# Moving the q and k transposes of an attention kernel from TensorE to the DMA crossbar

## The chip, the cores and the metric

One core of one Trainium2 chip. The metric is the device time of one execution in microseconds (us). A kernel is run several times; where a program runs on one core, a run counts as "slow" when it is over 1.5% above the fastest of its kernel, else as "fast".

## The reference

Two layers in one program. The attention (8 batches, 8 heads, 576 tokens, 64 features) adds a coarse attention over means of four tokens to a local one with a band of three neighbours on each side; its output x (4608 x 512) goes through a feed-forward layer with exact Gelu.

```python
q_d = q.reshape(B, H, S // 4, 4, D).mean(axis=3)         # k_d, v_d likewise
out_up = np.repeat(softmax_attention(q_d, k_d, v_d), 4, axis=2)
out_local = softmax_attention(q, k, v, mask=abs(i - j) < 4)
x = (out_up + out_local).transpose(0, 2, 1, 3).reshape(B * S, H * D)
out = gelu(x @ w_in) @ w_out                              # d_ff = 2048, float32 out
```

## The kernel before

All matmuls are fp16. The scores need q and k with the features on the partitions, so both are transposed. Before, each 256-byte row of a head is loaded for itself, with tokens on the partitions, and TensorE transposes blocks of 96 tokens x 2 heads against an identity into PSUM, from where VectorE copies them.

```python
def load_qk(b):                       # 2 x 6 DMAs, runs of 64 float32 = 256 bytes
    for nm, src in (("qn", q), ("kn", k)):
        for c in range(NCK):
            nc.gpsimd.dma_start(out=nat6(ld[b % 2][nm])[:, c, :, :],
                in_=src[b, :, CH * c:CH * c + CH, :].rearrange("h s d -> s h d"))
            yield
...
def t_in(b, p, which):                # one pair of heads
    nat = nat6(ld[b % 2]["qn" if which == "q" else "kn"])
    tr = ppool.tile([128, 1024], F16, tag="tr", name=f"tr_{which}")
    for c in range(NCK):
        nc.tensor.transpose(tr[:, CH * c:CH * c + CH], nat[:, c, 2 * p:2 * p + 2, :], I128[0:CH, 0:CH])
    if which == "q":
        nc.vector.tensor_copy(out=qT[:, p, :], in_=tr[:, 0:S])
        ...                           # GpSimd: sums of four tokens into qd
    else:
        ...                           # VectorE: two copies into kz, two sums into kdz
```

The feed-forward layer is woven into the attention. In each of nine chunks, `m1(c)` is 64 matmuls of the first product (16 groups of four, each closed by a Gelu on ACT; two PSUM banks take turns), and `m2(c)` is 64 of the second. The transposes of batch b = c + 1 stand between the matmuls of m1(c) ("first stage"), its attention between those of m2(c) ("second stage"); `f1(n)` and `f2(n)` issue the next n matmuls.

```python
elif b < B:
    v_down(b)                         # GpSimd: sums of four rows of v
    for p in range(NP):
        f1(6 if p == 0 else 7)
        t_in(b, p, "q")
        f1(7)
        t_in(b, p, "k")
    k_lo()
f1()
...                                   # attn(b, f2, ...), f2()
if b + 1 < B:
    run(load_qk(b + 1))
    run(load_v(b + 1))
```

The softmax here doesn't subtract the row's maximum and nothing guards it: scores larger than these inputs give would overflow.

## Time and profile before

| | before |
|---|---|
| time, median of the first 3 runs (lowest to highest) | 350.56 us (350.33 to 351.19) |
| span in the profile, mean granted clock | 348.4 us, 1.00 |
| TensorE busy | 97% of the span |
| one batch (first + second stage) | 15.89 + 20.33 = 36.22 us |

In the profile, PE is TensorE, PEld its weight loads, DVE VectorE, POOL GpSimd, SP the queue that issues DMAs. "The chain of waits" is followed back from the last instruction to what released it. L200 is a line of the kernel file. The lines themselves stand in the prediction below. The granted clock is the share of its full speed at which TensorE was let run. A DMA's landing is counted from its issue to the arrival of its last bytes. In the kernel, qT and kz hold the transposed q and k, qd and kdz their sums over four tokens, gT the results of Gelu, and out_sb what a store sends out.

### The profile page before, as it was taken

The numbers are of one execution on the slowest core, as the hardware profiler recorded it, in microseconds if no ns is written. First come the engines' busy times: TensorE is split into PE (matmuls) and PEld (weight loads), VectorE is DVE, ScalarE is ACT, GpSimd is POOL, SyncE is SP. The second block draws the span as 40 slices with busy tenths as digits, with TensorE's granted clock in tenths as the row PEclk, the third lists the DMA queues.
The fourth block names the chain that finished last, engine by engine and source line by source line (L and its number), as shares of the span: only waits on it lengthen the run. The fifth ranks groups of instructions, "written<-read, shape, count | busy, mean of one in ns | idle before, by whom it ended". The sixth has DMA issues, their size and how long they took to land.

```text
span 348.4 us, 7162 instructions
## 1 busy us (share of the span) xinstructions
PE 339.0 (97%) x2976; PEld 193.9 (56%) x2976; DVE 184.5 (53%) x338; ACT 192.8 (55%) x360; POOL 180.4 (52%) x243
## 2 busy tenths in 40 slices
PE   8898998999999999999999999999999999999996
PEld 4773455655665566555655575556655664444444
DVE  7793645747574857386747665676558470000000
ACT  3664465645764577357746764566556755614620
POOL 8957649633977298628963797369652000000000
PEclk9999999999999999999999999999999999999999
DMA  6999999920999099908990599129940001011002
GB/s 87 165 205 144 185 164 110 182 75 0 98 159 146 2 77 152 176 0 59 154 171 23 36 148 178 41 18 150 159 79 0 32 33 59 2 60 60 0 34 89
DMA packets 126543, 32.31 MB, mean 93 GB/s; under 512 B 109616, under 2 KB 122032, under 8 KB 126512
## 3 DMA queue, kind: packets, MB, share of 16 engines
q0 software_dynamic: 121184, 22.43, 82.2%
q1 hardware_dynamic: 5328, 9.44, 7.6%
q8 instruction: 23, 0.38, 0.4%
q14 instruction: 8, 0.07, 0.1%
HBM read 44.83 MB, written 9.44 MB: 156 GB/s over the span
## 4 chain that ended last, share of the span: by engine, by line
PE 88%; DMA 6%; DVE 2%; POOL 2%; issue 1%; ACT 0%; POOLq 0%
PE m_ps L224 35%; PE m_ps L200 33%; PE sc L348 4%; DMA w_in_sb<-in_moe_w_in_dram 3%; PE av L403 2%; PE tr_o L441 2%; DMA q_nat<-in_q_dram 2%; PE tr_k L237 2%; PE tr_q L237 2%; DMA k_nat<-in_k_dram 1%; DVE kz L272 1%; PE av L397 1%; PE sc L353 1%; PE m_ps L215 1%; PE av L395 1%; DVE kdz L275 1%
## 5 line engine op out<-in xcount | busy, mean ns | idle before, releaser
L200 PE MATMUL m_ps<-xT,w_in_sb 128*128 128x512 f16 x568 | 133.3, 379 | 0.5 <-ACT gT L195 0.5
L224 PE MATMUL m_ps<-w_out_sb,gT 128*128 128x512 f16 x560 | 130.3, 379 | 0.0
L203 ACT ACTIVATE gT<-m_ps 128x512 f16<-128x512 f32 x142 | 84.8, 597 | 56.7 <-PE m_ps L200 56.7
L200 PEld LDWEIGHTS <-w_in_sb 128*128 128x128 f16 x568 | 52.1, 97 | 54.7 <-issue 0.8
L224 PEld LDWEIGHTS <-gT 128*128 128x128 f16 x560 | 51.9, 98 | 54.6
L228 ACT COPY out_sb<-m_ps 128x512 f32<-128x512 f32 x35 | 20.6, 589 | 42.8 <-PE m_ps L224 37.8
L243 POOL TENSOR_TENSOR q_t<-qT 128x288 f32<-128x288 f16 x24 | 16.0, 667 | 52.0 <-DVE qT L240 37.8
L104 POOL DMA_DIRECT2D q_nat<-in_q_dram x42 | 32.6, 789 | 8.1 <-DMA w_out_sb<-in_moe_w_out_dram 5.7
L252 DVE TENSOR_REDUCE kdz<-kz 64x144 f16<-64x576 f16 x48 | 35.9, 747 | 1.5
L445 DVE TENSOR_TENSOR xT<-tr_o,xd 128x576 f16<-128x576 f16 x28 | 21.2, 758 | 26.9 <-ACT xd L444 26.9
L104 POOL DMA_DIRECT2D k_nat<-in_k_dram x42 | 32.2, 778 | 6.3 <-DMA w_in_sb<-in_moe_w_in_dram 3.5
L418 DVE TENSOR_TENSOR nall<-av,rr 128x896 f16<-128x896 f32 x29 | 31.7, 1091 | 1.0
L248 DVE COPY kz<-tr_k 64x576 f16<-64x576 f16 x48 | 21.9, 455 | 18.2 <-PE tr_k L237 17.5
L381 DVE TENSOR_TENSOR e<-e,band 128x1152 f16<-128x1152 f16 x28 | 21.0, 751 | 17.6 <-ACT e L375 17.6
L219 DVE COPY out_sa<-m_ps 128x256 f32<-128x256 f32 x2 | 0.8, 424 | 54.9 <-PE m_ps L215 54.9
L116 POOL DMA_DIRECT2D v_win<-in_v_dram x30 | 26.6, 912 | 0.0
L348 PE MATMUL sc<-qT,kz 128*128 128x112 f16 (+1 forms) x320 | 25.6, 214 | 0.0
L373 ACT ACTIVATE e<-sc 128x680 f16<-128x680 f32 x32 | 23.4, 732 | 2.0 <-PE sc L348 2.0
L348 PEld LDWEIGHTS <-kz 128*128 128x128 f16 x320 | 21.6, 97 | 0.9
L311 POOL TENSOR_TENSOR v_t<-v_grp 128x1024 f32<-128x1024 f16 x6 | 12.7, 2118 | 17.0 <-DMA v_grp<-in_v_dram 17.0
L444 ACT COPY xd<-tr_o 128x144 f16<-128x144 f16 x28 | 7.7, 276 | 22.0 <-PE tr_o L441 22.0
L375 ACT ACTIVATE e<-sc 128x472 f16<-128x472 f32 x32 | 18.2, 569 | 0.0
(168 smaller groups left out, 407.6 us busy)
## 6 DMA issues: line engine op xcount, KB each, us to landing
out_dram<-out_sb SPq DMA_DIRECT2D x35, 256.0 KB, 3.2
v_win<-in_v_dram POOLq DMA_DIRECT2D x40, 128.0 KB, 9.6
q_nat<-in_q_dram POOLq DMA_DIRECT2D x42, 96.0 KB, 3.7
k_nat<-in_k_dram POOLq DMA_DIRECT2D x42, 96.0 KB, 4.2
v_grp<-in_v_dram POOLq DMA_DIRECT2D x6, 512.0 KB, 8.8
w_in_sb<-in_moe_w_in_dram POOLq DMA_DIRECT2D x4, 512.0 KB, 8.1
w_out_sb<-in_moe_w_out_dram POOLq DMA_DIRECT2D x4, 512.0 KB, 9.4
v_lo<-in_v_dram POOLq DMA_DIRECT2D x6, 64.0 KB, 8.8
```

The lines of the kernel that those rows point to most:

```text
L104: nc.gpsimd.dma_start(out=nat6(ld[b % 2][nm])[:, c, :, :], in_=src[b, :, CH * c:CH * c + CH, :].rearrange("h s d -> s h d"))
L116: nc.gpsimd.dma_start(out=L["vw"][:, j, :, 0:64], in_=v[b, :, W0[j]:W0[j] + 128, :].rearrange("h s d -> s h d"))
L200: nc.tensor.matmul(out=ps, lhsT=w_in_sb[:, fc, 128 * j:128 * j + 128], rhs=xT[:, fc, 512 * c:512 * c + 512], start=(fc == 0), stop=(fc == 3))
L203: nc.scalar.activation(out=g[:, j, :], in_=ps, func=ACTF.Gelu)
L224: nc.tensor.matmul(out=ps, lhsT=g[:, j, 128 * t:128 * t + 128], rhs=w_out_sb[:, j, :], start=(j == 0), stop=(j == NJ - 1))
L248: nc.vector.tensor_copy(out=kz[r, p, hh, :], in_=tr[r, 0:S])
L252: nc.vector.tensor_reduce(out=kdz[r, p, hh, :], in_=kz[r, p, hh, :].rearrange("p (g r) -> p g r", r=4), axis=AX.X, op=ALU.add)
L348: nc.tensor.matmul(out=dst, lhsT=kz[:, p, hh, W0[j]:W0[j] + 128], rhs=qT[:, p, Q0[j]:Q0[j] + QW[j]], start=(b > 0), stop=True)
L373: nc.scalar.activation(out=e2[:, :, 0:340], in_=sc2[:, :, 0:340], func=ACTF.Exp, scale=0.125)
L381: nc.vector.tensor_tensor(out=e2, in0=e2, in1=band.unsqueeze(1).broadcast_to([128, 2, S]), op=ALU.mult)
L418: nc.vector.tensor_tensor(out=nall.rearrange("p j a c -> p a j c"), in0=av4[:, :, :, 0:64], in1=rr.unsqueeze(3).broadcast_to([128, 2, 7, 6 ...
L445: nc.vector.tensor_tensor(out=xT[:, p, S * b:S * b + S].rearrange("p (g r) -> p g r", r=4), in0=tr[:, 0:S].rearrange("p (g r) -> p g r", r=4),
```

## The change

The intent: take the 48 groups of transposes of batches 2 to 7 off TensorE, the bound, and replace 256-byte loads by 1.5 KB ones. Each partition now loads six consecutive tokens of a head (1536 bytes). VectorE regroups them so that a block of 128 columns is two heads of one of the six tokens. One DMA crossbar transpose each for q and k (a DMA that transposes what it moves) turns the whole 96 x 3072 array. Copies then bring the columns into token order: ACT does two of q's four, GpSimd two, VectorE all of k's. The transposes get the SP queue for themselves; the stores, all but the last two, move to ACT's. gT gets one buffer in place of two to make room.

```diff
+    def load_raw(b):
+        for nm, src in (("kn", k), ("qn", q)):
+            nc.gpsimd.dma_start(
+                out=RAW[nm][:, 0:3072].rearrange("p (h x) -> p h x", h=H),
+                in_=src[b].rearrange("h (p r) d -> p h (r d)", r=6))
+    def regroup(nm, p):               # VectorE, RAW -> REG, one pair of heads
+        ...
+    def cross(nm):
+        dst = kP if nm == "kn" else qP
+        nc.sync.dma_start_transpose(out=dst.rearrange("p r a t -> p (r a) t"), in_=REG[nm][:, 0:3072])
...
-        g = wpool.tile([128, NJ, 512], F16, tag="gT", bufs=2, name="gT")
+        g = wpool.tile([128, NJ, 512], F16, tag="gT", bufs=1, name="gT")
...
-                    nc.sync.dma_start(out=out[r0:r0 + 128, :], in_=osb)
+                    nc.scalar.dma_start(out=out[r0:r0 + 128, :], in_=osb)
...
-    def t_in(b, p, which): ...
+    def k_in(p):
+        for hh in range(2):
+            r = slice(64 * hh, 64 * hh + 64)
+            nc.vector.tensor_copy(out=kz[r, p, hh, :].rearrange("p (t r) -> p r t", r=6), in_=kP[r, :, p, :])
+        ...
+    def q_in(p, cp):
+        cp(out=qT[:, p, :].rearrange("p (t r) -> p r t", r=6), in_=qP[:, :, p, :])
...
 (attention of batch b, after av(b, p) and mask(p + 1))
+            if b + 1 < B:
+                nm = "kn" if p < 2 else "qn"
+                for i in range(2):
+                    regroup(nm, 2 * (p % 2) + i)
+                if p % 2:
+                    cross(nm)
...
 (first stage of batch b)
+            if b + 1 < B:
+                load_raw(b + 1)
             for p in range(NP):
-                f1(...); t_in(b, p, "q"); f1(7); t_in(b, p, "k")
+                if p < 2:
+                    f1(8)
+                q_in(p, nc.scalar.copy if p < 2 else nc.gpsimd.tensor_copy)
+                k_in(p)
+            for p in (2, 3, 0, 1):
+                q_sums(p)
             k_lo()
             v_down(b)
+            if b + 1 < B:
+                run(load_v(b + 1))
```

More of the change, by code (lines that the diff above doesn't have):

```diff
@@ L57 @@
     qT = cpool.tile([128, NP, S], F16, tag="qT", name="qT")
+    qP = cpool.tile([128, 6, NP, CH], F16, tag="qP", name="q_turned")
+    kP = cpool.tile([128, 6, NP, CH], F16, tag="kP", name="k_turned")
     qd = cpool.tile([128, NP, Sd], F16, tag="qd", name="qd")
@@ L104, in load_qk @@
                 nc.gpsimd.dma_start(
-                    out=nat6(ld[b % 2][nm])[:, c, :, :],
+                    out=nat6(ld[b][nm])[:, c, :, :],
                     in_=src[b, :, CH * c:CH * c + CH, :].rearrange("h s d -> s h d"))
@@ L122, in run @@
             pass
+    RAW, REG = ld[0], ld[1]
+    def load_raw(b):
[4 more added lines that the diff above has]
+    def regroup(nm, p):
+        nc.vector.tensor_copy(
+            out=REG[nm][:, 0:3072].rearrange("p (r h d) -> p r h d", r=6, h=H)[:, :, 2 * p:2 * p + 2, :],
+            in_=RAW[nm][:, 0:3072].rearrange("p (h r d) -> p r h d", r=6, h=H)[:, :, 2 * p:2 * p + 2, :])
+    def cross(nm):
+        dst = kP if nm == "kn" else qP
+        nc.sync.dma_start_transpose(out=dst.rearrange("p r a t -> p (r a) t"), in_=REG[nm][:, 0:3072])
     def load_qk8(b, h0, h1):
@@ L228, in m2 @@
                     nc.scalar.copy(out=osb, in_=ps)
-                    nc.sync.dma_start(out=out[r0:r0 + 128, :], in_=osb)
+                    nc.scalar.dma_start(out=out[r0:r0 + 128, :], in_=osb)
                 yield
-    def t_in(b, p, which):
-        nat = nat6(ld[b % 2]["qn" if which == "q" else "kn"])
-        tr = ppool.tile([128, 1024], F16, tag="tr", name=f"tr_{which}")
-        for c in range(NCK):
-            nc.tensor.transpose(tr[:, CH * c:CH * c + CH], nat[:, c, 2 * p:2 * p + 2, :],
-                                I128[0:CH, 0:CH])
-        if which == "q":
-            nc.vector.tensor_copy(out=qT[:, p, :], in_=tr[:, 0:S])
-            qg = qT[:, p, :].rearrange("p (g r) -> p g r", r=4)
-            t2 = wpool.tile([128, Sd, 2], F32, tag="qt2", bufs=2, name="q_t2")
-            nc.gpsimd.tensor_tensor(out=t2, in0=qg[:, :, 0:2], in1=qg[:, :, 2:4], op=ALU.add)
-            nc.gpsimd.tensor_tensor(out=qd[:, p, :], in0=t2[:, :, 0], in1=t2[:, :, 1], op=ALU.add)
-        else:
-            for hh in range(2):
-                r = slice(64 * hh, 64 * hh + 64)
-                nc.vector.tensor_copy(out=kz[r, p, hh, :], in_=tr[r, 0:S])
-            for hh in range(2):
-                r = slice(64 * hh, 64 * hh + 64)
-                with nc.allow_low_precision(reason="sums of four, kept in fp16 as before"):
-                    nc.vector.tensor_reduce(out=kdz[r, p, hh, :],
-                                            in_=kz[r, p, hh, :].rearrange("p (g r) -> p g r", r=4),
-                                            axis=AX.X, op=ALU.add)
@@ new lines, in k_in @@
+    def k_in(p):
+        for hh in range(2):
+            r = slice(64 * hh, 64 * hh + 64)
+            nc.vector.tensor_copy(out=kz[r, p, hh, :].rearrange("p (t r) -> p r t", r=6), in_=kP[r, :, p, :])
+        for hh in range(2):
+            r = slice(64 * hh, 64 * hh + 64)
+            with nc.allow_low_precision(reason="sums of four, kept in fp16 as before"):
+                nc.vector.tensor_reduce(out=kdz[r, p, hh, :],
+                                        in_=kz[r, p, hh, :].rearrange("p (g r) -> p g r", r=4),
+                                        axis=AX.X, op=ALU.add)
@@ L256, in t_in_g, with q_sums @@
+    def q_in(p, cp):
+        cp(out=qT[:, p, :].rearrange("p (t r) -> p r t", r=6), in_=qP[:, :, p, :])
+    def q_sums(p):
+        qg = qT[:, p, :].rearrange("p (g r) -> p g r", r=4)
+        t2 = wpool.tile([128, Sd, 2], F32, tag="qt2", bufs=2, name="q_t2")
+        nc.gpsimd.tensor_tensor(out=t2, in0=qg[:, :, 0:2], in1=qg[:, :, 2:4], op=ALU.add)
+        nc.gpsimd.tensor_tensor(out=qd[:, p, :], in0=t2[:, :, 0], in1=t2[:, :, 1], op=ALU.add)
     def t_in_g(b, p, which):
@@ L607 @@
         if b == 1:
+            load_raw(2)
+            run(load_v(2))
             f1(10)
@@ L615 @@
         elif b < B:
-            v_down(b)
-            for p in range(NP):
-                f1(6 if p == 0 else 7)
-                t_in(b, p, "q")
-                f1(7)
-                t_in(b, p, "k")
-            k_lo()
+            if b + 1 < B:
+                load_raw(b + 1)
+            for p in range(NP):
+                if p < 2:
[4 more added lines that the diff above has]
+                q_sums(p)
+            k_lo()
+            v_down(b)
+            if b + 1 < B:
+                run(load_v(b + 1))
         f1()
@@ L626 @@
             to_exp()
-            if b == 1:
-                attn(b, f2, 6, 9, 8)
-            else:
-                attn(b, f2, 6, 9, 9)
-        f2()
-        if b + 1 < B:
-            run(load_qk(b + 1))
-            run(load_v(b + 1))
+            attn(b, f2, 6, 9, 8 if b == 1 else 9)
+        f2()
 _INS = ['q', 'k', 'v', 'moe_w_in', 'moe_w_out']
```

## The prediction

> **What bounds the kernel now.** I read the page first, then the chain of waits in order of time, then the same two stretches as windows, then the timeline of each engine over one batch boundary.
>
> The page says that TensorE never rests and that the chain is TensorE almost throughout:
>
> ```profile
> PE 339.0 (97%) x2976; PEld 193.9 (56%) x2976; DVE 184.5 (53%) x338; ACT 192.8 (55%) x360; POOL 180.4 (52%) x243
> ...
> PE 88%; DMA 6%; DVE 2%; POOL 2%; issue 1%; ACT 0%; POOLq 0%
> ```
>
> The DMA part of the chain (6%) lies in the first 35 us, before the second batch; the change does not touch that start. From about 72 us on, each of batches 2 to 7 takes one period of 36.2 us: a first stage of 64 matmuls of the first product (L200) with the q and k transposes of the next batch between them, and a second stage of 64 matmuls of the second product (L224) with the attention between them. The chain through the head of one first stage (start, length, what):
>
> ```profile
> 108.69 1.29 PE m_ps L200 x6
> 109.98 0.26 PE tr_q L237 x6
> 110.24 1.51 PE m_ps L200 x7
> 111.75 0.26 PE tr_k L237 x6
> ```
>
> Each group of six transposes takes 0.26 us of TensorE's own time, and nothing waits around it. The same stage as a window, beside the first stage of the last chunk, which has no transposes in it (window, sum, then PE, PEld, DVE, ACT, POOL busy):
>
> ```profile
> 108.69:124.57 15.88, 15.88 (x113) 8.29 (x112) 10.88 (x21) 9.55 (x16) 7.28 (x13) 1.00 0.12 31
> 317.39:331.22 13.83, 13.83 (x66) 6.26 (x64) 0.00 (x0) 9.55 (x16) 0.00 (x0) 1.00 0.05 19
> ```
>
> The reader is to see 15.88 against 13.83 us at clock 1.00 in both: the transposes cost 2.05 us of path per batch, and ACT does the same 9.55 us in both. The DMA engines are heavily used but not on the path:
>
> ```profile
> q0 software_dynamic: 121184, 22.43, 82.2%
> ...
> q_nat<-in_q_dram POOLq DMA_DIRECT2D x42, 96.0 KB, 3.7
> ```
>
> So the transfers that become cheaper give nothing by themselves.
>
> **What the Trainium skill says.** (1) "DMA: Bandwidth & Descriptors", section "Latency and other measured facts", gives a crossbar transpose 261 GB/s with a non-contiguous middle dimension, and its section "Anatomy of one DMA" gives a fixed part of about 2.0 us per transfer on the GpSimd path. No run yet shows a crossbar transpose here. The trace of before agrees with a fixed part of that order: stores of 256 KB land in 2.0 us at the least. (2) The same page, "Issuing engines are not separate DMA queues": queues interleave on the same 16 engines, so the transpose will share them with loads that are in flight. (3) "SBUF — State Buffer", section "SBUF: two separate sides", says VectorE instructions in a two-port mode and GpSimd instructions exclude each other for a whole instruction. The new VectorE copies go SBUF to SBUF and may be of that kind; before, the same copies read PSUM, so the trace of before cannot show it.
>
> **The change part by part.**
>
> Removed from TensorE: batches 2 to 7, four head pairs, q and k, so 6 x 4 x 2 = 48 groups of six transposes. 48 x 0.26 = 12.5 us; the windows give 6 x 2.05 = 12.3. I take 12.4 us, all on the path.
>
> VectorE: the q copy (0.46 us x 24) goes away, kz copies stay with another source, and eight regroups per batch come in. A regroup of the prologue with 1024 elements takes 0.47 us; one of 768 I estimate at 0.41, so 3.3 us per batch, in a second stage where VectorE is busy 12.3 of 20.3 us. Hidden, but the last two set when q's transpose can start. The end of one attention, on VectorE:
>
> ```profile
> 104.48 0.24 DVE L417 RECIPROCAL rr<-av 128x14 f32<-128x14 f32 x1 [0.32 <-PE av L403]
> 104.76 1.09 DVE L418 TENSOR_TENSOR nall<-av,rr 128x896 f16<-128x896 f32 x1
> 107.95 0.76 DVE L445 TENSOR_TENSOR xT<-tr_o,xd 128x576 f16<-128x576 f16 x1 [2.10 <-ACT xd L444]
> ```
>
> The two regroups fit in the 2.10 us gap: 105.85 + 0.85 = 106.7, so q's transpose is issued at about 106.7 in this frame, 1.8 us before the next first stage starts its matmuls (108.52).
>
> ACT in the first stage: two q copies into token order, one after every eight matmuls. The engine has little room there, as only two PSUM banks take turns. The last first stage without transposes:
>
> ```profile
> 319.17 0.60 ACT L203 ACTIVATE gT<-m_ps 128x512 f16<-128x512 f32 x1 [0.28 <-PE m_ps L200]
> 320.03 0.60 ACT L203 ACTIVATE gT<-m_ps 128x512 f16<-128x512 f32 x1 [0.27 <-PE m_ps L200]
> ```
>
> The period is 0.863 us, Gelu takes 0.60, the idle rest is 0.27. A bank's four matmuls end (pipeline tail included) 0.2 us after the next bank's begin, so Gelu is done only about 0.07 us before its bank is wanted again (at the head of the stage: Gelu done at 110.18, bank wanted at 110.25). A copy of that size on ACT takes 0.64 us, some 0.55 net of the overlap with its neighbour:
>
> ```profile
> L561 ACT COPY qT<-m_ps x2: 641/642/644, 8.4 to 11.8; 128x576 f16<-128x576 f16 x2
> ```
>
> So each delays TensorE by 0.55 - 0.27 - 0.07 = 0.2 us: 12 copies, 2.4 us back on the path.
>
> Stores on ACT: 35 issues; on SP one took 0.33 us. In the attention ACT has gaps for them. The one at the head of a first stage (copy done at 109.31, first Gelu at 109.58) pushes that Gelu by about 0.15, past a slack of 0.07: 0.1 us x 6 = 0.6 us.
>
> The crossbar transposes: each moves 96 x 3072 fp16 = 590 KB. Estimate from the skill's figures: 590/261 = 2.26 us + 2.0 fixed + 0.3 issue, and 0.3 for sharing with the raw q load of the next batch, which is released at the same moment: 4.9 us. k's has about 12 us and is hidden. q's has from 106.7 to the moment ACT reaches its first q copy, after two Gelus: 111.05. That is 4.35 us. ACT then stands in order before the waiting transfer, and TensorE stops two banks later; with the slack gone, what is over 4.35 us is paid in full: 4.9 - 4.35 = 0.5 us x 6 = 3 us.
>
> gT with one buffer instead of two: free, I hold. The next chunk's first Gelu overwrites gT after matmuls that stand behind all the readers in TensorE's order.
>
> Sum: 350.6 - 12.4 + 2.4 + 0.6 + 3.0 = 344.2; I predict 344 us, 1.9% faster.
>
> **The rivals.**
>
> (a) The transpose is in time (4.3 us or less from issue to landing). Then the 3.0 falls away and the time is about 341, with even 339 if ACT's copies find more room than I give them. For it: the DMA queues have fewer small packets now (9216 of q and k per batch become 1536), so the engines are freer than the 82% says. Against: the raw q load starts at the same time.
>
> (b) The transpose is slow, 6.5 us and more, because its descriptors are made piece by piece or because it shares the engines evenly. Then ACT's wait replaces the transposes: 2.2 us or more per batch, 354 us at 6.5 + 0.5 for sharing, no gain at all.
>
> (c) GpSimd becomes the bound. After q has landed it does two q copies (about 0.7 us each by the q sums' rate), q sums 4 x 1.1 us, then the v sums:
>
> ```profile
> 105.16 2.12 POOL L311 TENSOR_TENSOR v_t<-v_grp 128x1024 f32<-128x1024 f16 x1 [2.92 <-DMA v_grp<-in_v_dram]
> 107.36 1.26 POOL L312 TENSOR_TENSOR v_d<-v_t 128x512 f16<-128x512 f32 x1
> ```
>
> 5.2 us with the three small ones. If q lands 3 us into the stage, that is 3 + 1.4 + 4.4 + 5.2 = 14 us, and the first attention product wants it at 13.8 + 5 = 18.8 us. A margin of 4.8 us; eight kz copies of about 0.45 us that exclude GpSimd take 3.6 of it. So I hold it hidden, narrowly; if not, 0 to 2 us per batch, up to 356.
>
> (d) VectorE late: its kz copies and sums are 4 x 2.4 = 9.7 us from the stage's start, wanted after 17 us. Unlikely.
>
> **Range and chances.** (a) gives 339 to 341.5, my middle 342 to 346, (b) and (c) 347 to 356. The length of the crossbar transpose decides it, and nothing in the profile shows it; I hold about even odds that it is short enough for over 2% (under 343.5). Range 338.5 to 352. Chances: faster 0.50, same 0.38, slower 0.12.
>
> **What would show it.** First-stage windows of 14.3 to 15.2 us in place of 15.88; at 13.9 my ACT terms are wrong, above 15.9 rival (b) or (c) holds. ACT's wait for the q copy, put down to the transpose's DMA: about 0.5 us each, six times. Issue to landing of the q transpose: 4.9 us. Before each first attention product no wait on the v sums by GpSimd. Attention stages still 20.3 us; if they grow, the stores on ACT or the regroups cost what I called hidden. If TensorE's idle time rests on Gelu with no DMA behind it, the ACT copies are dearer than 0.2 us. The prediction fails as a whole if the start before 72 us shifts, which I assume it does not.

## The result, and the profile after

| | before | after |
|---|---|---|
| median (lowest to highest) of 4 runs | 350.66 us (350.33 to 351.19) | 411.83 us (408.27 to 415.23) |
| ratio of fast runs, 95% interval | | 1.171 (1.161 to 1.181) |
| span and mean granted clock of the profiled run | 348.4 us, 1.00 | 406.6 us, 0.932 |

A ratio here is the mean time of one kernel's fast runs over that of the other's fast runs of the same rounds, so it is not quite the ratio of the medians. The change is 17% slower.

The page of the changed kernel, busy times and chain of waits:

```profile
PE 341.8 (84%) x2688; PEld 185.5 (46%) x2688; DVE 232.3 (57%) x362; ACT 214.0 (53%) x372; POOL 173.3 (43%) x195
...
PE 64%; DMA 22%; ACT 6%; DVE 4%; POOL 2%; issue 1%; SPq 0%; ACTq 0%; POOLq 0%
```

TensorE fell from 97% to 84% of the span, and DMA went from 6% to 22% of the chain. The pieces of the chain in order of time (start, length, what) name the transfer, once per batch:

```profile
71.58 19.58 DMA q_turned<-q_nat
...
124.70 15.10 DMA q_turned<-q_nat
...
172.96 11.20 DMA q_turned<-q_nat
184.24 2.10 ACT qT L266
...
217.33 10.67 DMA q_turned<-q_nat
...
261.43 12.29 DMA q_turned<-q_nat
...
306.48 6.26 DMA q_turned<-q_nat
```

These are q's crossbar transposes from issue to landing: 75.1 us in sum, where I had 4.9 each. One is short, 6.26 us. It is the one for batch 7, the only one that no load of a next batch accompanies. Behind each stands ACT's first copy into token order, 2.10 us where I had 0.64.

TensorE through the head of one first stage (start, length, engine, line, operation, output and inputs, count, in brackets the idle time before):

```profile
174.96 3.74 PE L221 MATMUL m_ps<-xT,w_in_sb 128*128 128x512 f16 x16
186.82 5.43 PE L221 MATMUL m_ps<-xT,w_in_sb 128*128 128x512 f16 x16 [8.13 <-ACT gT L224]
```

Sixteen matmuls run, filling two banks twice. Then TensorE waits 8.13 us for a Gelu, which waits behind ACT's q copy, which waits for the DMA. The second sixteen take 5.43 us, the first 3.74. The windows of such a restart, one batch earlier (the number after the five engines' busy times is the granted clock), say why:

```profile
142.45:146.00 3.55, 3.55 (x9) 1.32 (x9) 3.46 (x4) 2.86 (x3) 3.55 (x3) 0.50 0.00 0
146.00:150.00 4.00, 4.00 (x20) 1.75 (x18) 0.21 (x2) 2.74 (x5) 3.68 (x8) 0.98 0.00 0
```

For some 3.5 us after the wait the clock granted to TensorE was 0.50; it was 0.50 to 0.59 after each of the six waits of 5.8 to 12.0 us, and 1.00 after the one of 3.2 us (batch 7). The Trainium skill, "TensorE: Matmul & The Clock Gate", section "What's actually happening", has TensorE fall to half its clock after an idle window of about 3.4 us, and come back after as long a busy one. The trace agrees, and the prediction had left it out.

One period then adds up. From the head of one second stage to the next it is 154.79 to 199.16 = 44.37 us, against 36.22 before. The difference of 8.15 is -2.05 (transposes gone), +8.13 (the wait), and +2.0 (the 48 matmuls after it took 12.34 us in place of 48 x 0.2158 = 10.36). Over the kernel: TensorE waited 49.7 us for gT and 5.8 us for one output buffer, the stretches after the waits cost 10.3 us more than at full clock, and 12.4 us are gone. That is +53.4 of the 58.2 us by which the spans differ. Of the rest, 2.3 us lie in the 12 matmuls after the wait for the output buffer (4.92 us in place of 2.59), and 1.2 in the start: the head of batch 2's first stage moved from 72.29 to 73.49 us. Some 1.3 us are not placed.

### The profile page after: what moved, and what is told of

It reads as the page before. It is cut to its first block, busy times and chain, and to the rows that moved or that the text cites. A ratio compares the mean times of both kernels' runs of the same rounds, so it can differ in the third digit from the quotient of the medians.

```text
span 406.6 us, 6563 instructions
## 1 busy us (share of the span) xinstructions
PE 341.8 (84%) x2688; PEld 185.5 (46%) x2688; DVE 232.3 (57%) x362; ACT 214.0 (53%) x372; POOL 173.3 (43%) x195
## 4 chain that ended last, share of the span: by engine, by line
PE 64%; DMA 22%; ACT 6%; DVE 4%; POOL 2%; issue 1%; SPq 0%; ACTq 0%; POOLq 0%
PE m_ps L221 26%; PE m_ps L245 23%; DMA q_turned<-q_nat 18%; PE sc L366 4%; ACT qT L266 4%; PE av L421 2%; DMA v_win<-in_v_dram 2%; DMA k_turned<-k_nat 2%; PE tr_o L459 1%; DVE nall L436 1%; PE sc L371 1%; DVE kz L290 1%; PE m_ps L236 1%; ACT gT L224 1%; POOL v_win L153 1%; PE av L413 1%
## 5 line engine op out<-in xcount | busy, mean ns | idle before, releaser
L221 PE MATMUL m_ps<-xT,w_in_sb 128*128 128x512 f16 x568 | 139.0, 403 | 55.9 <-ACT gT L224 49.7
L221 PEld LDWEIGHTS <-w_in_sb 128*128 128x128 f16 x568 | 57.5, 102 | 132.4 <-issue 75.8
L224 ACT ACTIVATE gT<-m_ps 128x512 f16<-128x512 f32 x142 | 86.3, 613 | 42.8 <-PE m_ps L221 41.5
L257 DVE COPY kz<-k_turned 64x576 f16<-64x576 f16 x48 | 68.1, 1419 | 10.9 <-DMA k_turned<-k_nat 9.8
L266 POOL COPY qT<-q_turned 128x576 f16<-128x576 f16 x12 | 33.2, 2914 | 81.7 <-DMA q_turned<-q_nat 81.7
L266 ACT COPY qT<-q_turned 128x576 f16<-128x576 f16 x12 | 25.2, 2104 | 41.7 <-DMA q_turned<-q_nat 41.7
L366 PE MATMUL sc<-qT,kz 128*128 128x112 f16 (+1 forms) x320 | 26.6, 216 | 0.0
L391 ACT ACTIVATE e<-sc 128x680 f16<-128x680 f32 x32 | 23.4, 732 | 1.8 <-PE sc L366 1.8
L271 POOL TENSOR_TENSOR q_t<-qT 128x288 f32<-128x288 f16 x24 | 21.9, 911 | 0.0
L132 POOL DMA_DIRECT2D q_nat<-in_q_dram x6 | 4.6, 774 | 31.5 <-DVE q_nat L137 29.4
## 6 DMA issues: line engine op xcount, KB each, us to landing
k_nat<-in_k_dram POOLq DMA_DIRECT2D x6, 576.0 KB, 10.4
```

The lines of the kernel that those rows point to most:

```text
L221: nc.tensor.matmul(out=ps, lhsT=w_in_sb[:, fc, 128 * j:128 * j + 128], rhs=xT[:, fc, 512 * c:512 * c + 512], start=(fc == 0), stop=(fc == 3))
L224: nc.scalar.activation(out=g[:, j, :], in_=ps, func=ACTF.Gelu)
L257: nc.vector.tensor_copy(out=kz[r, p, hh, :].rearrange("p (t r) -> p r t", r=6), in_=kP[r, :, p, :])
L266: cp(out=qT[:, p, :].rearrange("p (t r) -> p r t", r=6), in_=qP[:, :, p, :])
L271: nc.gpsimd.tensor_tensor(out=t2, in0=qg[:, :, 0:2], in1=qg[:, :, 2:4], op=ALU.add)
L366: nc.tensor.matmul(out=dst, lhsT=kz[:, p, hh, W0[j]:W0[j] + 128], rhs=qT[:, p, Q0[j]:Q0[j] + QW[j]], start=(b > 0), stop=True)
```

## The experiments

Theory S: the transposes are long because they share the DMA engines with the loads that run beside them, and ACT stands in order before their landing. Theory I: a crossbar transpose of this size is long by itself. Under both lies a second question, what the copies into token order cost. Each run went beside runs of the kernel before on the same chip; the chip was not the same for all runs, so ratios compare better than times.

**1. The raw load of q moved behind GpSimd's q copies** (e1_qload_late)

```diff
-                load_raw(b + 1)
+                load_raw(b + 1, "k")
             for p in range(NP): ...   # q_in, k_in
+            if b + 1 < B:
+                load_raw(b + 1, "q")
```

> Edit: the raw load of q for the next batch is issued after GpSimd's two q copies, so it can no longer run beside the q transpose. Theory S (the q transposes are long because they share the DMA engines with that load): the six q transposes go from 19.6, 15.1, 11.2, 10.7, 12.3, 6.3 us to 6.3 to 7 us each, the first to about 10 as the raw k load is still beside it; about 34 us fewer on the path, 375 to 380 us. Theory I (a crossbar transpose of this size is long by itself): all six stay where they are and the time stays at 408 to 415 us.

Measured: 407.38 us, ratio 1.158 (1.153 to 1.163): a miss for theory S as I had put it. The q transposes took 6.6 to 13.6 us, median 12.1. But k's median went from 9.5 to 16.9 us: the later q load pushed the v loads onto k's transpose (issued until 199.8 us in one batch, and k's transpose at 200.8), and q's stood behind k's in the SP queue, which one q transpose held for 9.2 us at the median, against 3.8 in the changed kernel. The one load that I had blamed was not the cause alone.

**2. q transposed once only** (e2_q_once; wrong result, though within the tolerance of the comparison)

```diff
-                if p % 2:
+                if p % 2 and (nm == "kn" or b == 1):
                     cross(nm)
```

> Edit: q is transposed for batch 2 only; batches 3 to 7 reuse it (wrong result on purpose). If the loss lies in the wait for q's transpose: five waits of 55 us in sum are gone, the first of 19.6 us stays, 352 to 358 us. If the wait only hides another bound (VectorE's kz copies of 1.1 to 2.9 us with the kdz sums, which also end late in the stage): a wait for kz or KL takes its place and the time stays above 370 us.

Measured: 377.27 us, ratio 1.073. 35 us less, but not the 352 to 358 that the wait alone would give: under it was a second layer. In the period looked at, the chain now ran through k's transpose (10.8 us) and then VectorE's kz copies and sums, up to the first scores.

**3. Copies that write in order** (e3_write_order)

```diff
-        cp(out=qT[:, p, :].rearrange("p (t r) -> p r t", r=6), in_=qP[:, :, p, :])
+        cp(out=qT[:, p, :].rearrange("p (t r) -> p t r", r=6), in_=qP[:, :, p, :].rearrange("p r t -> p t r"))
```

(and likewise for kz)

> Edit: the copies into token order walk in the order of the output (contiguous writes, strided reads) instead of the order of the input (contiguous reads, writes 12 bytes apart). If the strided two-byte writes make them slow: ACT's q copy from 2.10 to about 0.65 us, VectorE's kz copy from 1.12 to 0.45-0.65, GpSimd's from 3.0 to about 0.8; the first ACT copy of each of six batches is on the path, so 9 to 15 us less, 396 to 403 us. If it is the SBUF source or the stride as such: the durations stay within 15% and the time stays at 408 to 415 us.

Measured: 415.61 us, ratio 1.181 (1.177 to 1.186). The durations did what the first theory said, in good part. ACT's copy in the changed kernel, and then in this one (ns, least, median, most):

```profile
L266 ACT COPY qT<-q_turned x12: 2097/2103/2117, 91.2 to 315.7; 128x576 f16<-128x576 f16 x12
```

```profile
L266 ACT COPY qT<-q_turned x12: 1162/1174/1262, 90.9 to 322.8; 128x576 f16<-128x576 f16 x12
```

kz went from 1.12 to 0.64 us, GpSimd's copy from 3.0 to 1.16. The time did not fall, which was a miss: the six landings of q grew from 75.1 to 85.2 us in sum, and ACT's waits for them from 41.7 to 49.1. Why the landings grew stays open.

**4. The kernel before, with one gT buffer and ACT's stores only** (e5_before_parts)

> Edit on the kernel before: only gT with one buffer and the stores issued by ACT. If these two parts are free, as predicted but for 0.6 us: 350.6 to 351.5 us. If they cost on their own (Gelu waiting for gT, or ACT held up by 35 issues of 0.34 us): 353 us or more, with TensorE waiting on ACT in the first stage.

Measured: 351.20 us, ratio 0.998 (0.995 to 1.001). In the kernel before, these two parts are free. Even the 0.6 us that I had charged the stores is not seen.

**5. No loads beside the transposes** (e6_no_loads; wrong result)

```diff
-            if b + 1 < B:
-                load_raw(b + 1)
...
-            if b + 1 < B:
+            if b + 1 == 3:
                 run(load_v(b + 1))
```

> Edit: q, k of batches 3 to 7 and v of batches 4 to 7 are not loaded at all (wrong result on purpose), so from batch 3 on the transposes meet only the stores. After the first four runs, theory S is widened: a transpose shares the DMA engines with whatever load is in flight, also with the other transpose. S: the five q transposes of batches 3 to 7 take 6.0 to 7.5 us, k's 5 to 6.5 us, TensorE's wait for each q shrinks to 2 to 3 us, time 372 to 382 us (the slow kz and q copies stay). Theory I (long by itself): q transposes of 10 us and more, time above 395 us.

Measured: 369.33 us, ratio 1.050, a little under the range of theory S. The landings of q's six transposes (us, least, median, most), in the changed kernel and then in this one:

```profile
DMA to landing us min/median/max: 6.3/11.7/19.6
```

```profile
DMA to landing us min/median/max: 5.3/5.8/6.4
```

k's median was 5.8 us as well. Theory I falls: the same transposes, alone but for the stores, take half as long at the median. ACT's waits for q fell from 41.7 to 8.2 us in sum, TensorE's for gT from 49.7 to 18.5; the slow copies of experiment 3 are still in this run. In the changed kernel one such window (172.5 to 184.5 us) shows the two at once; lines of the DMA queues (packets, MB, share) and of the landings:

```profile
q0 software_dynamic: 1429, 1.07, 66.6%
q1 hardware_dynamic: 2368, 0.59, 40.2%
...
q_nat<-in_q_dram POOLq DMA_DIRECT2D x1, 576.0 KB, 12.3
...
q_turned<-q_nat SPq DMA_TRANSPOSE x1, 11.2
```

Load and transpose start 0.15 us apart and land 1.3 us apart; a 256 KB store was in flight too. With no transpose beside it the raw q load took 7.0 us (median of e1_qload_late), and without loads the transpose took 5.8: together about the sum, 12.8. The transpose moves its 0.59 MB in 2368 packets of some 250 bytes; whether the size of the packets or the bytes decide how the two share was not tested.

**6. q transposed once, and the write order** (e7_q_once_order; wrong result)

> Edit: q transposed for batch 2 only (wrong result on purpose) and the copies write in order. Without the order this was 377 us, with kz copies and the ACT copies on the chain. If the strided writes are the second layer of the loss, under the wait: kz no longer on the chain, each ACT copy costs about 0.8 us, one first wait of 15 us: 353 to 360 us. If the second layer is something else (lock between VectorE and GpSimd, late k transposes): above 366 us.

Measured: 360.41 us, ratio 1.025 (1.020 to 1.030, so "unclear" at 2%), just past the upper edge of the first theory, and 17 us below e2_q_once. So the writes 12 bytes apart were the second layer; k's transposes, as late as there (median 9.7 us against 9.6), were not. With neither wait nor slow writes, a batch takes 35.2 us (ACT's first q copy at 125.16, 160.34 and 195.52 us): 1.0 us of the 2.05 is kept. The stage's chain runs through the two ACT copies of about 1.2 us and the Gelus behind them; they take the other half. Batch 2's transpose, which took 16.5 us to land and held ACT for 7.7, is still in the total.

**7. The first q copy on ACT after 40 matmuls in place of 8** (e8_late_use; write order, all of k's copies and the v sums ahead of the q copies)

```diff
-                    f1(8)
+                    f1(8 if p else 40)
```

> Edit: copies in write order, the v sums ahead of the q copies on GpSimd, and ACT's first q copy after 40 matmuls of the stage in place of 8, the second after 48. The transposes are not made faster. If the loss is ACT standing before a transfer that is not in yet (place of use): the slack of 4.35 us becomes about 11, with landings of 11 to 17 us some 25 us of waits remain of 85: 360 to 378 us. If the wait just moves to another engine (GpSimd's q sums too late for the first scores): above 395 us.

Measured: 370.78 us, ratio 1.046 (1.037 to 1.055) from its two fast runs, 365.28 and 370.30. That is 45 us less than with the write order alone, with q's median landing hardly shorter (14.1 us against 14.8; this profile fell in a slow run). ACT's waits for q (us in sum, times, longest), with the write order alone and then in this run:

```profile
ACT qT L266 <- DMA q_turned<-q_nat: 49.1, 6, 12.6
```

```profile
ACT qT L266 <- DMA q_turned<-q_nat: 16.1, 4, 7.4
```

TensorE's waits for gT fell from 51.8 to 20.2 us with them. GpSimd's new order was not tried by itself here, but in neither of the two runs does TensorE wait for GpSimd's v sums. So the place of use is a large part of the mechanism.

**8. Earlier transposes, loads behind them** (e10_early; write order, q copies all on GpSimd)

```diff
-                nm = "kn" if p < 2 else "qn"; two regroups per p; cross after p = 1 and p = 3
+                p = 0: all four regroups of k, cross;  p = 1: all four of q, cross   (batch 3 on)
...
+            k_in(p) x4;  q_in(p, nc.gpsimd.tensor_copy) x4
+            load_raw(b + 1);  q_sums x4;  k_lo();  v_down(b);  load_v(b + 1)
```

> Edit: meant as the version that beats both. Copies in write order; no q copy on ACT (GpSimd does all four); regroups and transposes of k in the first, of q in the second head pair of the attention, in place of k in the second and q in the fourth; the raw loads of the next batch behind GpSimd's q copies, so behind q's landing. q then has some 12 us from issue to the stage and GpSimd some more. By the sharing theory the transposes land in 6 to 11 us, before the stage: TensorE does not wait, 339 to 346 us, with a few us lost in batch 2 at the loaded start. If the crossbar transposes cannot be hidden whatever the slack, or VectorE and GpSimd exclude each other too long: above 355 us.

Measured: 380.04 us, ratio 1.082: a miss. q landed at 11.7 us median, k at 13.7: GpSimd came so late to the v loads (issued 179.1 to 185.1 us in one batch) that they met k's transpose (183.8 us), and q's queued behind. GpSimd did its v sums last, and TensorE waited 22.2 us for them in sum.

**9. The same, with the v sums first on GpSimd** (e11_early_v)

```diff
+            v_down(b)
             k_in(p) x4;  q_in(p, nc.gpsimd.tensor_copy) x4
             load_raw(b + 1);  q_sums x4;  k_lo()
-            v_down(b)
             load_v(b + 1)
```

> Edit: as the early version (380 us), but with the v sums ahead of the q copies on GpSimd, as in that run TensorE waited for v sums that GpSimd did after a late q. If that GpSimd order was the loss: q's wait now hides v's sums, 345 to 360 us. If q's landing itself is too late even so (12 to 15 us because k and q queue behind each other beside the v loads): still above 362 us, with GpSimd's q copies waiting for the transpose and TensorE for q's sums.

Measured: 353.14 us, ratio 1.004 (1.001 to 1.008). The same bytes, the same transposes, the same queues as in the change, and 59 us less. Five edits are in this number: the write order, no copy on ACT, earlier transposes, later loads, and the v sums first. The write order alone had gained nothing on the change (e3_write_order), and the v sums alone are worth 27 us (against e10_early); the other three were not tried apart. q's landings (us), and a first stage of this run as a window:

```profile
DMA to landing us min/median/max: 5.4/6.0/6.5
```

```profile
151.31:165.24 13.93, 13.93 (x65) 6.27 (x64) 13.50 (x18) 9.54 (x16) 13.61 (x17) 1.00 0.81 122
```

No wait, clock 1.00, 13.93 us in place of 15.88: the 2 us per batch are really there. The attention gives them back: from batch 2's first stage to batch 7's, a batch takes 36.2 us as before. Batch 2's first stage also begins 5.0 us later than before (77.26 against 72.29 us). The chain in the longest of these attention stages, 23.4 us in place of 20.33:

```profile
97.01 1.09 DVE nall L436
98.10 0.66 DVE e L399
98.76 4.08 DVE k_nat L137 x4
102.84 0.67 DVE xT L463
103.70 1.10 DVE nall L436
```

Four regroups in a row took 4.08 us while GpSimd did v's sums (2.0 to 2.4 us in later batches), and the output transposes waited for VectorE. The same four for q, with GpSimd through with its sums, took 1.15 us. The Trainium skill, "SBUF — State Buffer", section "Who interferes with whom", lets a copy in a two-port mode and a GpSimd instruction block each other whole; this fits it, though I did not test the pair by itself.

**10. k alone by the crossbar, q as before** (e9_k_only)

```diff
+            load_raw(b + 1, "k");  v_down(b)
+            for p in range(NP):
+                k_in(p);  f1(14 if p else 10);  t_in_q(b, p)        # q: TensorE, as before
+            k_lo();  regroup("kn", p) x4;  cross("kn");  q loads;  v loads
```

> Edit: only k goes by 1.5 KB runs, regroup and crossbar (copies in write order); q keeps its 256-byte loads and its TensorE transposes. k's regroup and transpose are issued in the first stage right after the kz copies, before q's and v's loads start, so with 20 us of slack; no new copy on ACT. 24 of 48 groups of transposes go: 24 x 0.26 = 6.2 us. If the loss of the full change is sharing plus place of use, k lands in 6 to 9 us, nobody waits for it, and the time is 344 to 347 us, faster than both. If a crossbar transpose costs in itself (held-up stores, VectorE and GpSimd excluding each other): 352 us or more.

Measured: 352.18 us, ratio 1.003 (0.998 to 1.007): a miss against 344 to 347, on the side of the second case. k landed in 10.4 us and more, not in 6 to 9, but with its long slack nobody waited for it from batch 3 on, and a batch took 35.3 us. The profile, of a slow run, shows a loss at the head of batch 2, in one piece of the chain:

```profile
67.34 13.92 DMA out_dram<-out_sb
```

A store took 13.92 us among the loads, and the two-deep output buffer held ACT for 9.5 us. Whether the fast runs lose the same there is not shown.

**11. The same with four output buffers, and k's regroup for batch 2 split over two head pairs** (e13_k_only_osb)

> Edit on the k-only version (352.2 us): four buffers for the stores' tiles in place of two, and k's regroup of batch 2 split over two head pairs. In the k-only run each later batch took 35.2 us in place of 36.2, as expected, but at the head of batch 2 ACT waited 9.5 us for a store of the first chunk that took 13.9 us to land among the loads, and TensorE with it. If that one store was all that ate the gain: 343 to 346 us, faster than before by 1.5 to 2%. If the loaded start holds batch 2 up by another way (k's first transpose, 16.6 us, then VectorE's kz copies and the first scores): 348 us or more.

Measured: fast runs 349.45, 347.37 and 350.15 us, ratio 0.994 (0.990 to 0.998), and three slow runs of 354 to 360. That falls short of 343 to 346. In the fast run that was profiled the wait for a store is gone, but k's first transpose still keeps VectorE waiting 4.9 us in batch 2. Which of the two edits did what is not separated. The result is inside 2%, so no clear winner over the kernel before, and the slow half of its runs is worse.

**12. The change with its stores back on SP** (e4_stores_sp)

> Edit: the changed kernel with the output stores back on SP, in one queue with the transposes. If the store queue is no part of the loss: 405 to 416 us. If stores on ACT cause part of it (a store waiting on ACT, or its transfers beside the transposes): below 403 us. If transposes then stand behind stores in order: above 418 us.

Measured: 410.91 us, ratio 1.170: as the change. The store queue is no part of the loss.

## Why the prediction was wrong

It said 344 us, 338.5 to 352; it was 411.8. By its own steps:

- *Transposes off TensorE, 12.4 us*: right. The first stages of e11_early_v are 13.93 us.
- *The crossbar transpose, 4.9 us*: **this step failed.** It was built as 2.26 + 2.0 + 0.3, and 0.3 for sharing. Without loads it takes 5.8 us (e6_no_loads), so the first three terms were 1.2 us short. The sharing term, 0.3 us, was 5 to 9 us in batches 3 to 6: load and transpose end together, after about the sum of their times. The one for batch 2, beside k's transpose and both loads, took 19.6 us in all. I had written that the load is released at the same moment and that the queues interleave, and then charged it 0.3. e11_early_v shows it the other way round: with the loads moved off the transposes, q lands in 6.0 us and TensorE's first stages run without a wait.
- *"What is over 4.35 us is paid in full"*: the mechanism was right. In the period shown ACT reached its copy 4.5 us after the issue. TensorE stopped two banks later and paid 8.13 us: 6.7 us is what the landing of 11.2 was over that, and the dearer copy (2.10 us for 0.64) is about the rest.
- *The clock*: missing from the sum. After waits of 5.8 to 12.0 us the granted clock was 0.50 to 0.59 for some 3.5 us; behind the waits for q this cost 10.3 us in all.
- *The copies into token order, on ACT 0.64 us and 0.2 us of path each*: mis-sized. 2.10 us as built, 1.17 when they write in order. I took the duration from a copy that read PSUM and wrote in order. e7_q_once_order shows the pair costs about 1 us per batch even at 1.2 us each. GpSimd's copies took 3.0 us where I had 0.7, VectorE's kz copies 1.12 and more where I had 0.45.
- *Stores on ACT, one gT buffer*: free in the kernel before (e5_before_parts), and the queue of the stores no part of the loss after (e4_stores_sp).
- *Regroups 0.41 us, hidden but for the last two*: right, at 0.35 us. q's last two are on the chain for 0.54 us before each transpose. Four at a time beside v's sums they are not hidden (e11_early_v).
- *Rivals*: (b), ACT's wait in place of the transposes, is what came, but I sized it at 354 and gave "slower" 0.12. By my own terms, 6.5 us gives 354, and with the 0.5 for sharing it should have read 357. (c) and (d), GpSimd and VectorE late, were real as the layer beneath: TensorE waited for GpSimd's v sums in e10_early, and with q's wait gone but for batch 2, kz copies of 1.12 us and more held the first scores (e2_q_once).
- *The start before 72 us does not shift*: nearly right, it came 1.2 us later. The loss of batch 2 came after it, where two transposes, two loads and stores were in flight together: TensorE waited 5.8 us for an output buffer and 8.6 for gT, and ACT's first q copy ran at 91.2 us.

## What to carry to other kernels

A DMA that was bandwidth in the background becomes latency on the path once an engine waits for it with other work behind: estimate it with everything that will be in flight beside it, and ask what the same buffer release also starts. Here the same bytes took 353 us with the transfer issued early, the loads behind it and the use late (and the copies and v sums in better order), and 412 us without; the price of waiting was the wait plus the slow clock after it. Neither this nor k alone beat the kernel before by 2%. When a transform leaves data in another order, try the reorder with strided reads and writes in order (here 2.10 us became 1.17 on ACT), and take its duration from a like access, not from a like size.

## What the Trainium skill lacked or had wrong

- "DMA: Bandwidth & Descriptors" has no time for the landing of a crossbar transpose of this size. My estimate from its 261 GB/s (section "Latency and other measured facts") and the 2.0 us fixed part of the GpSimd path (section "Anatomy of one DMA") is 4.3 us for 590 KB; the runs show 5.3 to 6.4 us with stores alone beside it, SBUF to SBUF. For how long a transpose holds its issuing queue it has cycle counts of earlier generations, but no time and nothing on loads beside it: 3.0 to 3.7 us per q transpose here without loads, 9.2 us at the median where transposes met loads (e1_qload_late).
- The same page, section "Issuing engines are not separate DMA queues", says that queues interleave, without a size: a transpose of some 2368 small packets beside a 1.5 KB-run load and a store lands at 10.7 to 15.1 us in place of 5.8, and the load at about 12 in place of 7.0.
- "ScalarE: Activation LUTs", section "What ACT_TABLE_LOAD costs", gives an ACTIVATE one element per cycle and lane, 0.83 ns, with no word on strides: a copy of 576 fp16 elements that writes 12 bytes apart took 2.10 us, 3.65 ns per element, and 1.17 us when the stride was on the read side. The pages on SBUF and on GpSimd warn of strided access, but give no cost for writes by ACT or GpSimd (GpSimd's copy: 3.0 and 1.16 us).
